# First layernorm of a spectral block: variances from the rows that the first DFT stage reads, instead of from a separate copy of x

## Chip, cores, metric

One core of one Trainium2 chip. The metric is the device time of one launch in microseconds. The kernel before takes 1050.82 us (median of 3 runs, 1050.31 to 1052.5).

## The reference

```python
def _layernorm(x, axis=-1, eps=1e-5):
    m = jnp.mean(x, axis=axis, keepdims=True)
    v = jnp.var(x, axis=axis, keepdims=True)
    return (x - m) / jnp.sqrt(v + eps)

def _A_ref(x, w_r, w_i):                 # x is (1, 2048, 1024), bf16
    X = jnp.fft.rfft2(x.astype(jnp.float32), axes=(-2, -1))
    X = X * (w_r + 1j * w_i)
    return jnp.fft.irfft2(X, s=(S, D), axes=(-2, -1)).astype(jnp.bfloat16)

x = A_x
x = x + _A_ref(_layernorm(x), A_w_r, A_w_i)
x = x + _B_ref(_layernorm(x), B_w1, B_b1, B_w2)    # two matmuls with an activation between
x = x + _A_ref(_layernorm(x), A_w_r, A_w_i)
x = x + _B_ref(_layernorm(x), B_w1, B_b1, B_w2)
```

Only the first layernorm and the first stage of the first spectral layer are changed. The transforms are matmuls with DFT matrices. The normalization by a row's standard deviation is put into the DFT matrix of the first stage: each of 128 groups of rows gets its own scaled copy of the matrix M0 (tile MN).

## The kernel before

Its prologue loads x (4 MB, tile XS, also the residual of later) and then the same rows once more in the order of the transform (tile XR, four quarters of 1 MB in pieces of 256 bytes). It takes the row statistics from XS, transposes them, scales, and runs stage one (an "eviction" copies a result of TensorE out of a pair of PSUM banks):

```python
    def first_scales(self):
        for j in range(0, 16, 4):          # row statistics, shared by VectorE and ScalarE
            n = 2 if j % 8 else 3
            for i in range(n):
                self.stats_dve(j + i)
            for i in range(n, 4):
                self.stats_act(j + i)
            self.sums_to_mv(j + n, 4 - n)
        self.root(0, 16)
        ...                                # spread, transpose on TensorE, copy back: tile RT

    def scaled(self, j):                   # 8 scaled copies of M0 for tile j, one by one
        for q in range(8):
            n = 8 * j + q
            if q % 3 == 1:
                self.op(self.act, lambda e, n=n: e.activation(self.MN.ap[:, n, :], self.M0.ap, ACT.Copy, scale=rc[:, n:n + 1]), ...)
            else:
                self.op(self.dve, lambda e, n=n: e.tensor_scalar(self.MN.ap[:, n, :], self.M0.ap, rc[:, n:n + 1], None, op0=ALU.mult), ...)

    def s1(self, li):
        for j in range(4 if not li else 0):
            self.scaled(j)
        for j in range(16):
            ps, banks, _ = self.pair()     # one of four pairs of PSUM banks
            ...                            # 8 matmuls of 128x128 per tile
            # eviction to Y: odd tiles on ScalarE, even ones on VectorE
            if not li and j + 4 < 16:
                self.scaled(j + 4)
```

Stage two begins when all 16 tiles are in Y; it runs in steps, and each of its first steps needs a block of the filter (w_r and w_i), which GpSimd loads while the steps go on.

## Time and profile before

| | before |
|---|---|
| time, median (us) | 1050.82 |
| profiled execution: time, span, granted clock | 1051.39, 1049.6, 0.966 |
| stage two starts (us from the span's start) | 46.24 |
| rest of that execution, time minus start of stage two | 1005.15 |

The page's strips of tenths (forty slices of 26 us; busy share of each engine, then the granted clock and the DMA engines) show the stretch at stake, the first two digits:

```profile
PE   0799489999999999999959967999999999999998
DVE  6898562531343100043326856426011100000111
ACT  6898263331000333300008844533300013340000
PEclk9699789999999999999989987999999999999999
```

In the first slice TensorE does nothing while VectorE and ScalarE take statistics; in the second its clock is granted at six tenths. The closer views, the chain and the durations of single instructions, are those that the prediction quotes.

### The profile page before, as it was taken

How to read it: one execution, taken by the hardware profiler on the slowest of the kernel's cores; microseconds unless marked ns; L12 is line 12 of the kernel's file. 1: busy time of each engine (PE TensorE's matmuls, PEld its weight loads, DVE VectorE, ACT ScalarE, POOL GpSimd, SP SyncE). 2: the span in 40 equal slices, each digit the busy share in tenths (PEclk: the TensorE clock that was granted, in tenths of full speed). 3: DMA queues.
4: the chain of work that ended last, by engine and by line, in shares of the span. 5: the costliest groups of instructions: out<-in, count | busy, mean ns of one | idle time of the engine just before them, and what ended most of it. 6: DMA issues, size and time to landing. Idle time of an engine off the chain costs nothing.

```text
span 1049.6 us, 14096 instructions
## 1 busy us (share of the span) xinstructions
PE 952.5 (91%) x5944; PEld 511.7 (49%) x6033; DVE 350.8 (33%) x776; ACT 336.5 (32%) x503; POOL 71.0 (7%) x114
## 2 busy tenths in 40 slices
PE   0799489999999999999959967999999999999998
PEld 0567465444444444444427746644444444444443
DVE  6898562531343100043326856426011100000111
ACT  6898263331000333300008844533300013340000
POOL 3242000000000000002421200000000000000000
PEclk9699789999999999999989987999999999999999
DMA  9779812464111221001941784145611112200000
GB/s 281 176 257 281 221 44 91 151 200 134 50 52 37 69 64 39 1 21 71 178 83 44 222 210 131 42 151 166 209 25 45 45 63 81 61 1 11 21 21 31
DMA packets 152718, 107.01 MB, mean 102 GB/s; under 512 B 74288, under 2 KB 131888, under 8 KB 152656
## 3 DMA queue, kind: packets, MB, share of 16 engines
q1 hardware_dynamic: 139936, 75.99, 25.4%
q0 software_dynamic: 9632, 28.45, 9.5%
q10 hardware_dynamic: 3088, 1.67, 0.6%
q8 instruction: 48, 0.79, 0.3%
q14 instruction: 14, 0.11, 0.0%
HBM read 80.85 MB, written 20.71 MB: 97 GB/s over the span
## 4 chain that ended last, share of the span: by engine, by line
PE 80%; DVE 9%; ACT 6%; DMA 3%; issue 1%; SPq 0%; ACTq 0%; DVEq 0%
PE PS L994 37%; PE PS L976 37%; DVE BN L459 2%; ACT ARENA L721 2%; PE PS L669 2%; DVE XS L915 1%; DVE ARENA L573 1%; DVE ARENA L790 1%; DMA u_scratch<-ARENA 1%; DMA ARENA<-u_scratch 1%; ACT ARENA L704 1%; DVE ARENA L951 1%; DVE ARENA L596 1%; PE PS L901 1%; ACT ARENA L792 1%
## 5 line engine op out<-in xcount | busy, mean ns | idle before, releaser
L976 PE MATMUL PS<-ARENA 128*128 128x512 bf16 (+1 forms) x1946 | 390.6, 360 | 10.3 <-DVE ARENA L951 7.2
L994 PE MATMUL PS<-ARENA 128*128 128x512 bf16 x1756 | 385.5, 379 | 1.9
L980 ACT ACTIVATE ARENA<-PS,B 128x512 bf16<-128x512 f32 (+1 forms) x248 | 159.8, 646 | 438.7 <-PE PS L976 438.7
L976 PEld LDWEIGHTS PS<-ARENA 128*128 128x128 bf16 x1984 | 194.2, 99 | 201.8 <-DVE ARENA L951 8.7
L994 PEld LDWEIGHTS PS<-ARENA 128*128 128x128 bf16 x1792 | 175.3, 98 | 211.5
L999 DVE TENSOR_TENSOR XS<-PS,XS 128x512 bf16<-128x512 f32 x64 | 44.3, 692 | 537.9 <-PE PS L994 537.9
L459 DVE BATCH_NORM_STATS2 BN<-XS 128x6 f32<-128x512 bf16 x104 | 67.2, 675 | 7.5 <-DMA XS<-in_A_x_dram 6.3
L915 DVE TENSOR_TENSOR XS<-PS,XS 128x512 bf16<-128x512 f32 (+1 forms) x40 | 29.1, 790 | 82.0 <-PE PS L901 82.0
L901 PE MATMUL PS<-MT,ARENA 128*128 128x32 bf16 (+1 forms) x768 | 24.5, 187 | 27.2 <-DMA ARENA<-u_scratch 23.8
L901 PEld LDWEIGHTS PS<-MT,ARENA 128*128 128x128 bf16 x768 | 23.0, 100 | 30.7 <-issue 24.7
L440 ACT ACTIVATE ARENA<-XS 128x1024 bf16<-128x1024 bf16 x24 | 25.3, 1055 | 36.4 <-DVE XS L915 31.5
L721 ACT ACTIVATE ARENA<-PS 128x1024 bf16<-128x1024 f32 x32 | 33.9, 1060 | 8.5 <-PE PS L717 8.5
L669 PE MATMUL PS<-FD,ARENA 128*128 128x256 bf16 (+1 forms) x256 | 33.6, 278 | 2.9 <-ACT ARENA L594 1.2
L750 ACT ACTIVATE ARENA<-PS 128x1024 bf16<-128x1024 f32 x32 | 33.9, 1061 | 3.7 <-PE PS L743 3.7
L249 POOL DMA_DIRECT2D xn_scratch<-ARENA x15 | 8.2, 550 | 390.7 <-DVE ARENA L498 390.7
L431 ACT ACTIVATE RS<-MV,EPS 128x1 f32<-128x1 f32 (+1 forms) x7 | 2.0, 292 | 98.5 <-DVE MV L462 96.2
L743 PE MATMUL PS<-ARENA 128*128 128x256 bf16 x256 | 33.2, 273 | 0.1
L743 PEld LDWEIGHTS PS<-ARENA 128*128 128x128 bf16 x256 | 24.5, 98 | 10.0 <-DVE ARENA L732 1.2
L725 DVE TENSOR_TENSOR ARENA<-ARENA 128x1024 bf16<-128x1024 bf16 x32 | 22.0, 687 | 21.9 <-ACT ARENA L721 21.9
L669 PEld LDWEIGHTS PS<-FD,ARENA 128*128 128x128 bf16 x256 | 24.5, 100 | 8.4 <-DVE ARENA L596 2.8
L764 PE MATMUL PS<-ARENA,BD 128*128 128x256 bf16 x192 | 25.9, 273 | 1.3 <-DVE ARENA L790 1.0
L498 DVE TENSOR_SCALAR ARENA<-XS,MV,RS 128x1024 bf16<-128x1024 bf16 x48 | 25.0, 543 | 1.0
(70 smaller groups left out, 503.8 us busy)
## 6 DMA issues: line engine op xcount, KB each, us to landing
ARENA<-in_B_w_dram SPq DMA_DIRECT2D x56, 512.0 KB, 3.9
ARENA<-in_B_w_dram SPq DMA_DIRECT2D x56, 256.0 KB, 4.2
u_scratch<-ARENA SPq DMA_DIRECT2D x14, 512.0 KB, 3.6
ARENA<-u_scratch SPq DMA_DIRECT2D x14, 512.0 KB, 5.7
XS<-in_A_x_dram SPq DMA_DIRECT2D x4, 1024.0 KB, 8.6
w_scratch<-ARENA POOLq DMA_DIRECT2D x8, 512.0 KB, 5.6
ARENA<-w_scratch POOLq DMA_DIRECT2D x8, 512.0 KB, 5.2
out_dram<-XS SPq DMA_DIRECT2D x16, 256.0 KB, 2.2
```

What stands on the lines that cost most here:

```text
L459: self.op(self.dve, lambda e: e.bn_stats(self.BN[:, j, 6 * h:6 * h + 6], self.XS[:, j, 512 * h:512 * h + 512]), reads=[self.r_xs[j]], part ...
L669: fns.append(lambda e: e.matmul(dst, at(r), FD[:, t:t + n], start=start, stop=stop))
L721: self.op(act, lambda e: e.activation(x.ap.rearrange("p a b -> p (a b)"), ps, ACT.Copy, scale=SIG), reads=banks, writes=[x.res])
L743: fns.append(lambda e, c=c, part=part: e.matmul(ps[:, c * 256:(c + 1) * 256], yk.ap[:, part, c * P:(c + 1) * P], t[:, (128, 0)[part]:(384, ...
L750: self.op(act, lambda e: e.activation(v.ap[:, :, i, :], src, ACT.Copy), reads=banks, parts=[v.res])
L764: fns.append(lambda e, dst=dst, part=part, c=c: e.matmul(dst, BD[:, c:c + P], mov(kd, part), start=(part == 0), stop=(part == 1)))
L901: fns.append(lambda e, l=l: e.matmul(ps[:, w * l:w * l + w], self.UT.ap[:, u0 + l, :], self.MT[:, 8 * lo:8 * lo + w], start=True, stop=True))
L915: self.op(self.dve, lambda e: e.tensor_tensor(xs, src, xs, ALU.add), reads=rb, parts=self.r_xs[lo:lo + nb])
L976: fns.append(lambda e, db=db, bank=bank, fl=fl: e.matmul(PS[:, bank, 0:w], wb.ap[:, db, fl * P:(fl + 1) * P], x.ap[:, db, tok], start=(db ...
L980: self.op(act, lambda e, bank=bank, ft=ft: e.activation(at.ap[:, ft, tok], PS[:, bank, 0:w], ACT.Mish, bias=self.B1[:, ft:ft + 1]), reads= ...
L994: fns.append(lambda e, i=i, ft=ft: e.matmul(PS[:, bank, :], at.ap[:, ft, t * P:(t + 1) * P], W2[ft].ap[:, h * 512:(h + 1) * 512], start=(i ...
L999: self.op(dve, lambda e: e.tensor_tensor(xs, PS[:, bank, :], xs, ALU.add), reads=[self.r_bank[bank]], writes=[self.r_xs[j]])
```

## The change

Its intent: the statistics need XS, but the rows themselves are also in XR. A block matrix of ones (BO, 8 by 8 blocks) lets TensorE add the eight pieces of each row across partitions, for the rows and for their squares. So x needn't come first, the 128 small scalings become 16 operations on VectorE, and each quarter of rows can start when it has landed. The residual x is loaded later: one megabyte behind the rows, the other three behind the first three steps of stage two (the "gate"). The core of the diff:

```diff
+                prog = (sp, self.pool, self.act)[h % 3] if q == 0 else (sp, self.pool)[h % 2]
...
+    def squares(self, q, prog):           # 4096 elements of XR squared into XQ
...
+    def sums(self, q, sq):                # 16 matmuls of 256 columns with BO, of the rows (sq=0) or their squares (1)
...
+        fns = [lambda e, i=i: e.matmul(ps, self.BO.ap, src[:, :, 8 * i:8 * i + 8], start=(i == 0), stop=(i == 15)) for i in range(16)]
...
+    def roots(self, q):                   # reduce, square, subtract on DVE; Sqrt on ACT; reciprocal on DVE
...
     def scaled(self, j):
+        self.op(self.dve, lambda e: e.tensor_tensor(self.MN.ap[:, n, :], self.M0.ap.unsqueeze(1).to_broadcast([P, 8, P]),
+                                                    self.RT.ap[:, n].unsqueeze(2).to_broadcast([P, 8, P]), ALU.mult), ...)
...
+    def s1_first(self):
...
+        self.sums(0, 0)
+        self.squares(0, dve)
+        self.sums(0, 1)
+        self.roots(0)
+        for j in range(16):
+            q = j // 4 + 1
+            if q < 4 and j % 4 == 0:
+                self.squares(q, act)
+                self.sums(q, 0)
+            self.scaled(j)
+            self.s1_mm(0, j, j % 3)
+            if q < 4 and j % 4 == 1:
+                self.sums(q, 1)
+            self.s1_evac(j, j % 3, dve if j in (13, 15) else act)
+            if q < 4 and j % 4 == 2:
+                self.roots(q)
...
+            if li == 0 and step < 3:      # in stage two
+                gate = Res("gate")
+                gate.set_w(self.pe, self.pe.count)
+                self.load_x(step + 1, [gate])
```

More of the change, by code (lines that the diff above doesn't have):

```diff
@@ L171, in make_tables @@
                 FD=np.concatenate(FD, axis=1), BD=np.concatenate(BD, axis=1), FT=by_group(FT), BT=by_group(BT),
-                ident=np.eye(P))
+                ident=np.eye(P), BO=np.kron(np.eye(16), np.ones((8, 8))))
 def to_bf16_bits(a):
@@ L307, in build @@
         self.con = {k: v.ap().bitcast(BF) for k, v in con.items()}
-        self.con["IDF"] = nc.inline_tensor(np.eye(P, dtype=np.float32), name="c_idf").ap()
         self.u_d = nc.dram_tensor("u_scratch", (8, P, 16, P), BF, kind="Internal").ap()
@@ L361, in layout @@
         K = 1024
-        self.o = dict(XR=0, Z=0, X=12 * K, T=20 * K, YK=28 * K, V=40 * K, JT=48 * K, M0=49 * K, IDF=49 * K + 256, RT=50 * K,
-                      JUNK=51 * K, WR=54 * K, YS=56 * K, UT=64 * K, MN=64 * K, Y=96 * K, XN=128 * K, U=128 * K,
+        self.o = dict(XR=0, Z=0, X=12 * K, T=20 * K, YK=28 * K, V=40 * K, JT=48 * K, M0=49 * K, BO=49 * K + 256, RT=50 * K, XQ=32 * K,
+                      ST=51 * K, WR=54 * K, YS=56 * K, UT=64 * K, MN=64 * K, Y=96 * K, XN=128 * K, U=128 * K,
                       FT=140 * K, BT=144 * K + 512, WT=self.W1_OFF)
@@ L375, in prologue, with load_small @@
         self.op(self.pool, lambda e: e.memset(self.EPS[:], 1e-5), writes=[self.r_eps, self.r_warm])
-        self.warm(ACT.Sqrt)
-        xt = self.x[0].rearrange("(t p) d -> p t d", p=P)
-        for c in range(4):
-            self.dma(sp, self.XS[:, 4 * c:4 * c + 4, :], xt[:, 4 * c:4 * c + 4, :], f"x{c}", writes=self.r_xs[4 * c:4 * c + 4])
         small = {}
-        def load_small(name, n, d):
-            b = self.alloc(name, self.o[name], [n], d)
-            self.dma(sp, b.ap, self.con[name], name.lower(), writes=[b.res])
+        def load_small(name, n, prog=sp):
+            b = self.alloc(name, self.o[name], [n])
+            self.dma(prog, b.ap, self.con[name], name.lower(), writes=[b.res])
             small[name] = b
-        load_small("M0", P, BF)
-        load_small("IDF", P, F32)
-        self.M0, self.IDF = small["M0"], small["IDF"]
         self.XR = self.alloc("XR", self.o["XR"], [P, P])
@@ L394, in prologue, with load_x @@
             for h in range(8):
-                prog = self.pool if q and h % 2 else sp
-                self.dma(prog, self.XR.ap[h:P:8, 32 * q:32 * q + 32, :], xv[h][:, 32 * q:32 * q + 32, :], f"xr{q}{prog.name}",
-                         parts=[r], reads=[self.r_xs[15]] if prog is self.pool else [])
+                prog = (sp, self.pool, self.act)[h % 3] if q == 0 else (sp, self.pool)[h % 2]
+                self.dma(prog, self.XR.ap[h:P:8, 32 * q:32 * q + 32, :], xv[h][:, 32 * q:32 * q + 32, :], f"xr{q}{prog.name}", parts=[r])
             self.r_xr.append(r)
-            if q == 2:
-                self.dma(sp, self.FD[:], self.con["FD"], "fd", writes=[self.r_fd])
-        load_small("JT", 4 * P, BF)
+            if q == 0:
+                load_small("BO", P, self.act)
+                load_small("M0", P, self.act)
+                self.warm(ACT.Sqrt)
+        self.M0, self.BO = small["M0"], small["BO"]
+        self.dma(sp, self.FD[:], self.con["FD"], "fd", writes=[self.r_fd])
+        load_small("JT", 4 * P)
         self.JT, self.r_jt = small["JT"].ap, small["JT"].res
         self.w1_next = 0
+    def load_x(self, c, after):
+        xt = self.x[0].rearrange("(t p) d -> p t d", p=P)
+        self.dma(self.sp, self.XS[:, 4 * c:4 * c + 4, :], xt[:, 4 * c:4 * c + 4, :], f"x{c}", reads=after,
+                 writes=self.r_xs[4 * c:4 * c + 4])
     def constants(self):
@@ L527, in pair, with copy @@
         return self.PS[:, 2 * i:2 * i + 2, :].rearrange("p a b -> p (a b)"), [self.r_bank[2 * i], self.r_bank[2 * i + 1]], 2 * i
-    def copy(self, prog, dst, src, reads, writes, scale=None):
+    def copy(self, prog, dst, src, reads, writes, scale=None, parts=()):
         if prog is self.act:
@@ L535, in copy @@
             fn = lambda e: e.tensor_copy(dst, src)
-        return self.op(prog, fn, reads=reads, writes=writes)
-    def first_scales(self):
-        dve, act = self.dve, self.act
-        for j in range(0, 16, 4):
-            n = 2 if j % 8 else 3
-            for i in range(n):
-                self.stats_dve(j + i)
-            for i in range(n, 4):
-                self.stats_act(j + i)
-            self.sums_to_mv(j + n, 4 - n)
-        self.root(0, 16)
-        rt = self.alloc("RT", self.o["RT"], [16, 8], F32)
-        self.op(dve, lambda e: e.tensor_copy(rt.ap, self.RS[:, 2, :].unsqueeze(2).to_broadcast([P, 16, 8])),
-                reads=self.r_rs, writes=[rt.res])
-        bank = self.r_bank[7]
-        self.group([lambda e: e.transpose(self.PS[:, 7, 0:P], rt.ap.rearrange("p a b -> p (a b)"), self.IDF.ap)],
-                   reads=[rt.res, self.IDF.res], writes=[bank])
-        self.op(dve, lambda e: e.tensor_copy(rt.ap.rearrange("p a b -> p (a b)"), self.PS[:, 7, 0:P]), reads=[bank], writes=[rt.res])
-        self.MN = self.alloc("MN", self.o["MN"], [P, P])
-        self.r_mn = [Res(f"mn{j}") for j in range(16)]
-        for r in self.r_mn:
-            r.inherit(self.MN.res)
-            r.begin()
-        self.RT = rt
@@ L564, in scaled, with open_scales @@
-    def scaled(self, j):
-        rt = self.RT
-        rc = rt.ap.rearrange("p a b -> p (a b)")
+        return self.op(prog, fn, reads=reads, writes=writes, parts=parts)
+    def open_scales(self):
+        self.XQ = [self.alloc(f"XQ{i}", self.o["XQ"] + i * 8192, [32, P]) for i in range(2)]
+        self.ST = self.alloc("ST", self.o["ST"], [4, 4, 32], F32)
+        self.RT = self.alloc("RT", self.o["RT"], [P], F32)
+        self.MN = self.alloc("MN", self.o["MN"], [P, P])
+        self.r_st, self.r_rt, self.r_mn = ([Res(f"{n}{i}") for i in range(k)] for n, k in (("st", 4), ("rt", 4), ("mn", 16)))
+        for b, rs in ((self.ST, self.r_st), (self.RT, self.r_rt), (self.MN, self.r_mn)):
+            for r in rs:
+                r.inherit(b.res)
@@ new lines, in squares @@
+    def squares(self, q, prog):
+        x, b = self.XR.ap[:, 32 * q:32 * q + 32, :], self.XQ[q % 2]
+        fn = (lambda e: e.activation(b.ap, x, ACT.Square)) if prog is self.act else (lambda e: e.tensor_tensor(b.ap, x, x, ALU.mult))
+        self.op(prog, fn, reads=[self.r_xr[q]], writes=[b.res])
+    def sums(self, q, sq):
+        bank = 6 + q % 2
+        ps = self.PS[:, bank, 256 * sq:256 * sq + 256].rearrange("p (n l) -> p n l", l=8)
+        src = self.XQ[q % 2].ap if sq else self.XR.ap[:, 32 * q:32 * q + 32, :]
+        fns = [lambda e, i=i: e.matmul(ps, self.BO.ap, src[:, :, 8 * i:8 * i + 8], start=(i == 0), stop=(i == 15)) for i in range(16)]
+        rb = self.r_bank[bank]
+        if not sq:
+            rb.begin()
+        w = list(rb.prev.items()) + self.BO.res.wait_r() + (self.XQ[q % 2].res if sq else self.r_xr[q]).wait_r()
+        t = None
+        for i, fn in enumerate(fns):
+            t = self.pe.add(fn, waits=w if i == 0 else (), inc=(i == 15))
+        self.mark(self.pe, t, reads=[self.BO.res] + ([self.XQ[q % 2].res] if sq else []), parts=[rb])
@@ new lines, in roots @@
+    def roots(self, q):
+        dve = self.dve
+        st, rst, rb = self.ST.ap[:, q], self.r_st[q], self.r_bank[6 + q % 2]
+        s1, s2, a, b = (st[:, i, :] for i in range(4))
+        rc = self.RT.ap[:, 32 * q:32 * q + 32]
+        src = self.PS[:, 6 + q % 2, :].rearrange("p (c n l) -> p c n l", c=2, l=8)
+        self.op(dve, lambda e: e.tensor_reduce(st[:, 0:2, :], src, axis=mybir.AxisListType.X, op=ALU.add), reads=[rb], writes=[rst])
+        self.op(dve, lambda e: e.tensor_tensor(a, s1, s1, ALU.mult), writes=[rst])
+        self.op(dve, lambda e: e.scalar_tensor_tensor(b, a, -1.0 / self.D, s2, ALU.mult, ALU.add), writes=[rst])
+        self.op(self.act, lambda e: e.activation(a, b, ACT.Sqrt, bias=self.EPS[:, 0:1], scale=1.0 / self.D), reads=[self.r_eps],
+                writes=[rst])
+        self.op(dve, lambda e: e.reciprocal(rc, a), reads=[rst], writes=[self.r_rt[q]])
@@ new lines, in scaled, with s1_mm @@
+    def scaled(self, j):
+        n = slice(8 * j, 8 * j + 8)
+        self.op(self.dve, lambda e: e.tensor_tensor(self.MN.ap[:, n, :], self.M0.ap.unsqueeze(1).to_broadcast([P, 8, P]),
+                                                    self.RT.ap[:, n].unsqueeze(2).to_broadcast([P, 8, P]), ALU.mult),
+                reads=[self.r_rt[j // 4], self.M0.res], writes=[self.r_mn[j]])
+    def s1_mm(self, li, j, i):
+        M, XR = self.M, self.XR
+        ps, banks = self.PS[:, 2 * i:2 * i + 2, :].rearrange("p a b -> p (a b)"), [self.r_bank[2 * i], self.r_bank[2 * i + 1]]
+        fns = []
@@ L567, in scaled @@
         for q in range(8):
             n = 8 * j + q
-            if q % 3 == 1:
-                self.op(self.act, lambda e, n=n: e.activation(self.MN.ap[:, n, :], self.M0.ap, ACT.Copy, scale=rc[:, n:n + 1]),
-                        reads=[rt.res, self.M0.res], parts=[self.r_mn[j]])
-            else:
-                self.op(self.dve, lambda e, n=n: e.tensor_scalar(self.MN.ap[:, n, :], self.M0.ap, rc[:, n:n + 1], None, op0=ALU.mult),
-                        reads=[rt.res, self.M0.res], parts=[self.r_mn[j]])
@@ L576, in s1, with s1_evac @@
-    def s1(self, li):
+            m = M[:] if li else self.MN.ap[:, n, :]
+            fns.append(lambda e, q=q, n=n, ps=ps, m=m: e.matmul(ps[:, q * P:(q + 1) * P], XR.ap[:, n, :], m, start=True, stop=True))
+        self.group(fns, reads=[self.r_xr[j // 4], self.r_m if li else self.r_mn[j]], writes=banks)
+    def s1_evac(self, j, i, prog):
+        ps, banks = self.PS[:, 2 * i:2 * i + 2, :].rearrange("p a b -> p (a b)"), [self.r_bank[2 * i], self.r_bank[2 * i + 1]]
+        self.copy(prog, self.Y.ap[:, :, 8 * j:8 * j + 8], ps.rearrange("p (q k) -> p k q", q=8), banks, [], parts=[self.Y.res])
@@ L577, in s1 @@
+    def s1_first(self):
+        self.open_scales()
         self.Y = self.alloc("Y", self.o["Y"], [P, P])
         self.Y.res.begin()
-        M, XR = self.M, self.XR
-        for j in range(4 if not li else 0):
-            self.scaled(j)
-        for j in range(16):
-            ps, banks, _ = self.pair()
-            fns = []
-            for q in range(8):
-                n = 8 * j + q
-                m = M[:] if li else self.MN.ap[:, n, :]
-                fns.append(lambda e, q=q, n=n, ps=ps, m=m: e.matmul(ps[:, q * P:(q + 1) * P], XR.ap[:, n, :], m,
-                                                                   start=True, stop=True))
-            self.group(fns, reads=[self.r_xr[j // 4], self.r_m if li else self.r_mn[j]], writes=banks)
-            src = ps.rearrange("p (q k) -> p k q", q=8)
-            dst = self.Y.ap[:, :, 8 * j:8 * j + 8]
-            if j % 2 or li and j == 8:
-                self.op(self.act, lambda e, dst=dst, src=src: e.activation(dst, src, ACT.Copy), reads=banks, parts=[self.Y.res])
-            else:
-                self.op(self.dve, lambda e, dst=dst, src=src: e.tensor_copy(dst, src), reads=banks, parts=[self.Y.res])
-            if not li and j + 4 < 16:
-                self.scaled(j + 4)
@@ L599, in s1 @@
-        for r in ([self.MN.res, self.M0.res] + self.r_xr if not li else []):
-            r.r(self.pe, self.pe.count)
-            self.XR.res.r(self.pe, self.pe.count)
+        act, dve = self.act, self.dve
+        self.sums(0, 0)
[7 more added lines that the diff above has]
+                self.sums(q, 0)
+            self.scaled(j)
+            self.s1_mm(0, j, j % 3)
[4 more added lines that the diff above has]
+                self.roots(q)
@@ new lines, in s1_first, with s1 @@
+        for r in [self.MN.res, self.M0.res, self.XR.res, self.BO.res] + self.r_xr + [b.res for b in self.XQ]:
+            r.r(self.pe, self.pe.count)
+        for r in (self.RT.res, self.ST.res, self.M0.res, self.XR.res, self.MN.res):
+            r.r(dve, dve.count)
+            r.r(act, act.count)
+    def s1(self, li):
+        if li == 0:
+            return self.s1_first()
+        self.Y = self.alloc("Y", self.o["Y"], [P, P])
+        self.Y.res.begin()
+        for j in range(16):
+            i = self.pair()[2] // 2
+            self.s1_mm(1, j, i)
+            self.s1_evac(j, i, self.act if j % 2 or j == 8 else self.dve)
@@ L640, in layer_A @@
         if li == 0:
-            self.junk = self.alloc("JUNK", self.o["JUNK"], [self.D])
-            self.first_scales()
-        if li == 0:
             self.open_tables(0)
             self.constants()
+            self.load_x(0, [])
         o, K = self.o, 1024
```

## The prediction

> **What bounds the kernel now.** The page first: TensorE is busy 91% of the span, and the two idle slices of the strip of tenths are at the start and around 540 us. The change touches only the first layernorm and the first stage of the first spectral layer, so I went from the page to the chain of waits and the timeline of the first 60 us. The chain, merged, of the kernel before:
>
> ```profile
> 0.74 5.50 DMA XS<-in_A_x_dram
> 6.27 1.30 DVE BN L459 x2
> ...
> 22.20 0.32 ACT RS L431
> ...
> 22.53 0.27 DVE RS L433
> ...
> 24.02 3.34 DVE ARENA L573 x20
> 27.36 1.13 DVE ARENA L596
> 28.49 1.62 DVE ARENA L573 x10
> ...
> 43.92 2.27 DVE ARENA L596 x2
> 46.20 0.05 issue
> 46.24 1.89 PE PS L669 x8
> ...
> 50.06 1.94 ACT ARENA L704 x2
> 52.00 0.77 ACT ARENA L885 x2
> 52.77 0.92 ACT ARENA L721
> ```
>
> Columns are start, duration, work. Until 22.8 us everything waits for row statistics (L459, bn_stats, DVE's share of them). From 24.0 to 46.2 DVE never stops: it scales the 128 copies of the DFT matrix (L573) and empties every second PSUM pair (L596). At 46.24 the second stage starts (L669), and from 50 us the chain runs through ScalarE's evictions, 0.92 us apart. So up to 46.24 the path is vector work and TensorE waits; after it each stage hangs on the one before. What the change is worth is the new start S of the second stage minus 46.24, plus any harm done later.
>
> Durations for the working come from these groups (busy us, mean ns) and from the stretches (PE, PEld, DVE, ACT, POOL busy, then granted clock, DMA share, GB/s):
>
> ```profile
> L440 ACT ACTIVATE ARENA<-XS 128x1024 bf16<-128x1024 bf16 x24 | 25.3, 1055 | 36.4 <-DVE XS L915 31.5
> L725 DVE TENSOR_TENSOR ARENA<-ARENA 128x1024 bf16<-128x1024 bf16 x32 | 22.0, 687 | 21.9 <-ACT ARENA L721 21.9
> L594 ACT ACTIVATE ARENA<-PS 128x1024 bf16<-128x1024 f32 x8 | 8.1, 1012 | 0.6 <-PE PS L588 0.6
> L596 DVE CAST ARENA<-PS 128x1024 bf16<-128x1024 f32 x8 | 9.6, 1212 | 0.0
> 20.00:25.00 5.00, 0.48 (x1) 0.18 (x1) 3.77 (x17) 2.07 (x7) 2.04 (x4) 1.00 1.18 236
> 35.00:40.00 5.00, 3.66 (x32) 3.02 (x31) 5.00 (x20) 5.00 (x15) 4.69 (x8) 0.50 1.00 134
> 50.00:55.00 5.00, 4.95 (x39) 3.64 (x38) 1.21 (x2) 4.94 (x7) 4.07 (x7) 1.00 0.65 182
> ```
>
> Two things to see. The spectral rows, read in 256-byte pieces, come in at about 240 GB/s with the DMA engines full (share 1.18). And TensorE's clock is granted at 0.50 in this phase although it is busy three quarters of the time; it comes back only after the dense start of stage two (0.68 in the microsecond from 49).
>
> **What the Trainium skill says.** "TensorE: Matmul & The Clock Gate", Part 1: the array runs at half clock until a window of some 3.4 us has been busy, and falls back after an idle one. The trace agrees and adds the threshold that matters here: 8 matmuls of 256 columns start 1.69 us apart per eight at 0.50 (0.211 each, from 46.24) and 0.87 per eight at 1.00 (0.109, from 55.98), and a window about half busy (29.2 to 32.6 us) was enough to lose the clock. "ScalarE: Activation LUTs", What ACT_TABLE_LOAD costs: 186 ns plus 0.833 ns an element; for 1024 elements 1.04, measured 1.055. "VectorE: DVE Perf Modes", The perf-mode tier table: a tensor_tensor reaches 2x in bf16 and 1x with fp32, a tensor_reduce 1x. The 0.687 us of L725 is the 2x rate; no fp32 tensor_tensor of this size is in the trace, so I take the 1x eviction's 1.21 us, next one after 1.13. "DMA: Bandwidth & Descriptors", Issuing engines are not separate DMA queues: three issuing engines save issue time only, which the full share above bears out.
>
> **The change part by part.** Removed: the 4 MB load of x ahead of the rows and all row statistics, 22 us on DVE and ScalarE, with the fp32 transpose. The 128 small scalings become 16 tensor_tensors of 1024 elements on DVE. Evictions go to ScalarE except numbers 13 and 15. Added: per quarter one squaring of 4096 elements (first on DVE, then ScalarE), 32 matmuls of 256 columns, a reduction, a root, a reciprocal. Moved: x is loaded behind the rows and in the first three steps of stage two.
>
> Costs: squaring on ScalarE 0.19 + 4096 x 0.833 ns = 3.6 us; on DVE 4 x 0.61 = 2.3 with L725's spacing. Sixteen sum matmuls 16 x 0.109 = 1.75 warm, 16 x 0.211 = 3.4 cold. Eight stage-one matmuls about 0.5 warm, 0.9 cold, plus 0.25 for the last one's tail and the semaphore. Reduction of 512 fp32 from PSUM, about 0.7 (half an eviction). The small ops up to the reciprocal 1.0 (in the kernel before 21.80 to 22.82). Scaling 1.2, next after 1.14. ScalarE eviction 0.93.
>
> *Start.* The first quarter is 1.05 MB, with two tables 1.11 MB; at 245 GB/s 4.5 us from about 2.3 us, so it is in SBUF at 7.2. Sums cold, the second sixteen half cold: 7.3 to 13.4. Reduction to 14.3, root done 15.0. First scaling 15.4. ScalarE has its first squaring (quarter 1) next in its queue: 15.0 to 18.6. Call this end X1. The other quarters land at about 11.5, 16 and 20 us and are waited for by nobody.
>
> *One quarter.* The order of instructions closes a ring. ScalarE's queue is: squaring q, three evictions, root q, one eviction, squaring q+1. From the end X of a squaring, warm: sums of squares, X+1.8; matmuls of the third group, X+2.5; its eviction, X+3.45; root (queued behind that eviction), X+3.8; reciprocal, X+4.1; the fourth scaling (queued behind the reciprocal on DVE), X+5.35; its matmuls, X+6.1; its eviction, X+7.05; squaring, X+10.6. Cold, 1.65 for sums and 0.4 to 0.5 for each matmul group more: X+13.2. ScalarE works only some 7.7 us of that; the rest is the ring. TensorE is dense for 3 us and idle for 3 us in turn, so I expect the clock to be lost and regained in each quarter: 11.6 as a mean. X2 = 30.2, X3 = 41.8.
>
> *End.* After X3: reciprocal 4.1, three scalings to 7.65, matmuls 8.4, DVE's copy 13 to 9.55, two scalings 11.9, matmuls 12.7, copy 15 to 13.9; cold 17.0. I take 14.7, so S = 56.5, which is 10.3 us later than 46.24.
>
> *Later.* The first gated megabyte of x is issued when step 0 of stage two ends, together with the filter load for step 2. Before, that load was issued at 49.57 and 50.28, landed in 3.3 to 3.7 us, at about 54.0, and its matmuls ran at 54.67: 0.6 us of slack. Sharing the DMA engines costs about 2 us there, of which ScalarE's backlog of nearly 1 us hides half: 1.0. Filter loads, tables and x in later steps fit into stretches like 58 to 61 us, where the DMA moved almost nothing. The rest of the program is shifted.
>
> Sum: 1050.8 + 10.3 + 1.0 = 1062.1.
>
> **The rivals.** *A gain.* If the quarters overlapped as intended, ScalarE's own work would be the bound: from 14.7 four roots (1.3), three squarings (10.6), 14 evictions (13.0), then DVE's last copy, S about 41.5 and 1046. For it speaks that 22 us of statistics are gone and the rows come 4 us into the program rather than last; against it the ring, which is in the order of the queues and not in the data. *All cold.* If TensorE never gets its clock, two cycles of 13.2 and the cold end give S = 18.6 + 26.4 + 17.0 = 62, and 1068; for it speaks 0.50 over 17 us before, against it the dense stretch of sums, which exceeds a window. *DMA as the bound.* If the first quarter came at 10 us because later quarters of other queues overtake it, S moves by those 3 us; the rows' total rate bounds the last quarter at 20 us, so no more. *Filter loads starved by x.* Should all three megabytes get ahead of loads for steps 2 and 3, 4 us more instead of 1.
>
> **Range and chances.** All warm and an early first quarter give S about 51.5 and 1056; a gain in the fixed hops or a squaring in another order of readiness takes off another 2 to 3. All cold with starved filter loads gives 1071. The range is 1053 to 1069. Two per cent is 21 us; a stage that lasted 46 us cannot give 21 by a reordering whose ScalarE work alone ends at 41, and a loss of 21 needs every rival of loss at once: 0.01 faster, 0.95 same, 0.04 slower.
>
> **What would show it.** In the changed profile: stage two (the matmuls on FD) starting at 54 to 59 us; squarings on ScalarE of 3.6 us spaced by 10.5 to 13; ScalarE waiting for TensorE before the third and fourth eviction of each quarter, about 3 us or more a quarter; DVE waiting for the root before its reciprocal; a scaling of 1.2 us (0.7 would mean the 2x rate); clock 0.5 and 1.0 in turn; the matmuls of the filter for step 2 a microsecond or so late. The prediction is wrong if squarings come every 8 us, or if the first sums start much before 7 us, or if a sum matmul, whose moving operand is read in 16-byte runs, takes another time than 0.109 and 0.211.

## The result, and the profile after

The changed kernel took 1064.51 us (median of 4 runs, 1061.64 to 1067.35) beside 1050.99 for the kernel before; the ratio is 1.0127, 95% interval 1.0097 to 1.0156. (Ratios and intervals are from the runs of the same rounds, so not quite the ratio of the quoted medians. For two kernels below they also differ from the ratio of the plain means of all listed executions, which is then given.) In the profiled execution (1064.61 us) stage two started at 57.34, 11.1 us later than before, and the rest took 1007.27, 2.1 us longer.

The chain of the changed kernel, merged: start, duration, work.

```profile
5.34 12.28 DMA ARENA<-in_A_x_dram
17.62 0.02 issue
17.64 3.62 ACT ARENA L554
...
21.32 1.92 PE PS L562 x16
23.24 0.46 PE PS L599 x8
...
23.72 1.02 ACT ARENA L533
24.74 0.22 ACT ARENA L582
...
24.98 0.35 DVE ARENA L584
25.34 1.09 DVE ARENA L588
...
26.47 1.05 PE PS L599 x8
27.52 0.02 issue
27.54 0.02 ACT ARENA L533
...
28.46 3.62 ACT ARENA L554
...
39.28 3.62 ACT ARENA L554
...
57.34 1.89 PE PS L707 x8
...
61.37 7.51 DMA ARENA<-in_A_w_i_dram
```

L554 is the squaring, L562 the sums, L599 stage one's matmuls, L533 the eviction, L582 the root, L584 the reciprocal, L588 the scaling. The reader sees the ring that the prediction wrote down, hop for hop: squaring, sums of squares, third group's matmuls, its eviction, root, reciprocal, fourth scaling, its matmuls, its eviction, squaring. It closes after 10.82 us, twice (17.64, 28.46, 39.28). The chain begins, however, not with a root but with a load: SyncE's seventh piece of rows, the last of its half of quarter 1, issued at 5.34, took 12.28 us. And behind stage two's start the chain runs through another load, of the filter.

The waits say the same, by who waits and for what (total us, times, longest):

```profile
ACT ARENA L554 <- DMA ARENA<-in_A_x_dram: 1.8, 1, 1.8
PE PS L912 <- DMA ARENA<-in_A_w_i_dram: 3.1, 1, 3.1
```

The second is TensorE's wait for the filter block of step 2. These are the landing times of that filter tensor's loads from 40 to 75 us, first of the kernel before, then of the changed kernel:

```profile
DMA to landing us min/median/max: 3.5/3.9/6.3
```

```profile
DMA to landing us min/median/max: 6.0/7.5/8.2
```

The changed kernel was run once more later, unedited, for the scatter of its profile:

> The changed kernel once more, unedited, beside the others of this call: 1064 to 1065, as in its first runs; it shows how far profile and time of one and the same kernel differ between runs (landing of the first rows and of quarter 1, wait for the filter).

It took 1063.86 us (1063.46 to 1066.29; ratio 1.0134, interval 1.0121 to 1.0147). In its profile the squarings came 10.82 and 10.40 apart, stage two started at 58.42 and the wait for the filter was 1.74 us. So the start of stage two scatters by a microsecond and that wait by more than one, between executions of one kernel.

### The profile page after: what moved, and what is told of

The parts are those of the page before. It is cut to its first block, busy times and chain, and to the rows that moved or that the text cites. A ratio compares the mean times of both kernels' runs of the same rounds, so it can differ in the third digit from the quotient of the medians.

```text
span 1062.5 us, 14272 instructions
## 1 busy us (share of the span) xinstructions
PE 966.3 (91%) x6071; PEld 522.9 (49%) x6160; DVE 341.3 (32%) x678; ACT 326.0 (31%) x443; POOL 72.8 (7%) x117
## 4 chain that ended last, share of the span: by engine, by line
PE 76%; DVE 7%; DMA 6%; ACT 5%; issue 3%; POOL 2%; SPq 0%; ACTq 0%; DVEq 0%; POOLq 0%
PE PS L1018 36%; PE PS L1036 32%; POOL ARENA L249 2%; PE PS L707 2%; DMA xn_scratch<-ARENA 1%; DVE XS L957 1%; DMA ARENA<-in_A_x_dram 1%; ACT ARENA L554 1%; DMA u_scratch<-ARENA 1%; ACT ARENA L533 1%; DVE ARENA L828 1%; ACT ARENA L759 1%; PE PS L781 1%; DMA ARENA<-u_scratch 1%; DVE ARENA L993 1%
## 5 line engine op out<-in xcount | busy, mean ns | idle before, releaser
L461 DVE BATCH_NORM_STATS2 BN<-XS 128x6 f32<-128x512 bf16 x84 | 54.7, 677 | 1.2
L759 ACT ACTIVATE ARENA<-PS 128x1024 bf16<-128x1024 f32 x32 | 33.3, 1042 | 8.6 <-PE PS L755 8.6
L788 ACT ACTIVATE ARENA<-PS 128x1024 bf16<-128x1024 f32 x32 | 33.3, 1041 | 4.1 <-PE PS L781 4.1
L781 PE MATMUL PS<-ARENA 128*128 128x256 bf16 x256 | 33.2, 273 | 0.5 <-DMA ARENA<-c_bt 0.4
L562 PE MATMUL PS<-ARENA 128*128 128x256 bf16 x128 | 19.4, 319 | 14.7 <-DMA ARENA<-in_A_x_dram 12.0
L533 ACT ACTIVATE ARENA<-PS 128x1024 bf16<-128x1024 f32 x23 | 22.4, 1027 | 25.4 <-PE PS L599 25.3
```

Source lines behind the costliest of these rows:

```text
L461: self.op(self.dve, lambda e: e.bn_stats(self.BN[:, j, 6 * h:6 * h + 6], self.XS[:, j, 512 * h:512 * h + 512]), reads=[self.r_xs[j]], part ...
L533: fn = (lambda e: e.activation(dst, src, ACT.Copy)) if scale is None else \
L759: self.op(act, lambda e: e.activation(x.ap.rearrange("p a b -> p (a b)"), ps, ACT.Copy, scale=SIG), reads=banks, writes=[x.res])
L781: fns.append(lambda e, c=c, part=part: e.matmul(ps[:, c * 256:(c + 1) * 256], yk.ap[:, part, c * P:(c + 1) * P], t[:, (128, 0)[part]:(384, ...
L788: self.op(act, lambda e: e.activation(v.ap[:, :, i, :], src, ACT.Copy), reads=banks, parts=[v.res])
```

## The experiments

Each run was timed in five rounds against the kernel before on the same chip. My theory after the first result had four parts: the order of the instructions around the ring (main part), the half clock of TensorE, the starved filter load, the late quarter 1. Each rival says that its part is hidden behind the others.

**One part at a time: order.** The root goes behind the fourth eviction instead of ahead of it, so that neither has to wait for the other's chain:

```diff
-            if q < 4 and j % 4 == 2:
+            if q < 4 and j % 4 == 3:
                 self.roots(q)
```

> One line: the root of the next quarter (reduction, root, reciprocal) is issued after the fourth eviction of a quarter, not after the third. No work is added or taken away. Ring theory (squaring, three evictions, root, reciprocal, fourth scaling, its matmuls, its eviction, next squaring): the fourth scaling no longer hangs behind the reciprocal, so the spacing of ScalarE's squarings falls from 10.8 us to about 8, stage two starts at about 50.5 instead of 57.3, and the time falls by about 7 us to 1057 to 1058. Rival (the work itself of ScalarE and DVE sets the quarter): spacing and time unchanged, 1064. Rival (TensorE's half clock sets the quarter): spacing falls by less than 1 us.

1060.71 us (1055.61 to 1061.36), ratio 1.0088 (1.0071 to 1.0105): a gain of 3.8, half of what I had expected; stage two started at 55.39, not 50.5. The squarings came 8.11 us apart once (17.82 to 25.93), which confirms the ring, and then 9.77. ScalarE's timeline and TensorE's (start, duration, then the idle time before and what ended it) show why:

```profile
25.93 3.62 ACT L554 ACTIVATE ARENA<-ARENA 128x4096 bf16<-128x4096 bf16 x1
29.44 1.94 ACT L533 ACTIVATE ARENA<-PS 128x1024 bf16<-128x1024 f32 x2
33.66 1.94 ACT L533 ACTIVATE ARENA<-PS 128x1024 bf16<-128x1024 f32 x2 [2.28 <-PE PS L599]
```

```profile
29.61 3.57 PE L562 MATMUL PS<-ARENA 128*128 128x256 bf16 x16
```

The sums of squares took 3.57 us where the changed kernel's took 1.92, because they now fall into a stretch at half clock, and ScalarE waited 2.28 us for the tile behind them instead of 0.63. The tail grew too: the matmuls of the last tiles came in two groups of 16 that took 2.17 us each. Two cycles of 8.11 would have saved 5.4 us; the second cycle and the tail (16.1 us from the end of the last squaring to stage two, where the changed kernel needed 14.4) took 3.3 of that back, by this reading through the clock; the runs that hold the clock test it below. (In the profiled executions only 2.0 us of the gain lie in the start of stage two. The wait for the filter was 1.7 us instead of 3.1, which is within its scatter.)

**x not gated.** All four loads of x are issued behind the constants; the gate is gone.

```diff
-            self.load_x(0, [])
+            for c in range(4):
+                self.load_x(c, [])
...
-            if li == 0 and step < 3:
-                gate = Res("gate")
-                gate.set_w(self.pe, self.pe.count)
-                self.load_x(step + 1, [gate])
```

> All four megabytes of x are issued right behind the small tables at about 24 us, with no wait for stage two; the DMA engines stand idle from 37 to 57 us in the changed kernel. Theory (the gated loads of x starve the filter load of step 2, TensorE waits 3.1 us there): stage two still starts at about 57, the wait for the filter goes from 3.1 us to below 0.5, the time falls by 2 to 3 us to about 1062. Rival (the loads are late whatever x does, or ScalarE's backlog hides the wait): within 0.5 us of 1064.5.

1061.95 us (1061.08 to 1062.57), ratio 1.0108 (1.0095 to 1.0121), as expected. Stage two started at 57.21, as in the changed kernel, and TensorE no longer waited for the filter. The landing times of the filter's loads from 40 to 75 us in this kernel:

```profile
DMA to landing us min/median/max: 3.8/4.5/5.0
```

So it was the gated x that starved them.

**Rows dealt by quarter.** Of quarter 1, seven of eight pieces go to GpSimd's queue, of quarter 2 five, and SyncE gets five of quarter 3:

```diff
-  ... if q == 0 else (sp, self.pool)[h % 2]
+  ... if q == 0 else (sp, self.pool)[h > 0 if q == 1 else h % 3 > 0 if q == 2 else h > 4]
```

> The same 32 row loads, with more of quarters 1 and 2 issued from GpSimd (7 of 8, 5 of 8) and more of quarter 3 from SP. Theory (SP's queue gets only half of the service that GpSimd's gets, so its four loads of quarter 1 land at 17.6 us, and ScalarE's first squaring waits 1.8 us for them): quarter 1 lands at about 13, the first squaring starts at 15.9 right behind the root, all later stages are 1.8 us earlier, time about 1062.7. Rival (the rows arrive at one total rate, and quarter 1 is late because quarter 0 was): first squaring still at about 17.6, no change.

1063.5 us (1062.38 to 1064.67), ratio 1.0123 (1.011 to 1.0137): no gain clear of the noise. ScalarE's timeline:

```profile
16.68 0.32 ACT L582 ACTIVATE ARENA<-ARENA,EPS 128x32 f32<-128x32 f32 x1 [11.62 <-DVE ARENA L581]
16.91 3.60 ACT L554 ACTIVATE ARENA<-ARENA 128x4096 bf16<-128x4096 bf16 x1
...
24.63 1.02 ACT L533 ACTIVATE ARENA<-PS 128x1024 bf16<-128x1024 f32 x1 [2.30 <-PE PS L599]
```

The wait for rows is gone: the squaring stands right behind the root. But the first rows landed at 9.74 instead of 8.67 in this execution, and the first cycle took 12.23 us, with a wait of 2.30 for TensorE where it had been 0.63: the sums of squares of that quarter took 3.35 us. In this execution, then, the wait that was removed came back as half clock; one execution does not show that it has to. Nor need the landing at 9.74 be the edit's doing: it was between 8.67 and 9.82 in the six profiles that deal the rows as the changed kernel does.

**All three together.**

> The three edits together. If the three losses lie one after the other on the path they add: 7 + 2.5 + 1.8 = 11.3 us, so about 1053, stage two from about 48.7. If one hides another, less: above 1055.

1057.89 us (1056.41 to 1058.74), ratio 1.0068 (1.0054 to 1.0081). From the changed kernel's 1064.51 the single gains are 3.8, 2.6 and 1.0 (the last within the noise), together 7.4; measured 6.6. The parts as measured nearly add up; what failed was the 11.3 that I had expected of them. 7 us of the loss remained. Stage two started at 54.09; the squarings were 9.75 and 8.11 apart. In the cycle of 9.75 the sums of squares took 3.25 us, in that of 8.11 they took 1.92.

**Holding the clock.** To test the clock by itself, matmuls of 512 columns whose result is overwritten are put where TensorE idles, into the PSUM bank that the next real matmuls start afresh:

```diff
+    def busy(self, i, n):
+        ps = self.PS[:, 2 * i, :]
+        w = self.r_xr[0].wait_r() + self.r_bank[2 * i].wait_w()
+        for k in range(n):
+            self.pe.add(lambda e: e.matmul(ps, self.XR.ap[:, 0, :], self.XR.ap[:, 0:4, :], start=True, stop=True), ...)
...
             self.scaled(j)
+            self.busy(j % 3, {3: 10, 7: 10, 11: 10, 14: 9}.get(j, 0))
             self.s1_mm(0, j, j % 3)
...                                        # and busy(1, 5) ahead of stage two
```

> The changed kernel as it is, with idle-time matmuls of 512 columns whose result is thrown away: ten ahead of the first-stage matmuls of tiles 3, 7 and 11, nine ahead of tile 14, five ahead of stage two. Theory (TensorE's half clock lengthens what lies on the path: sums of squares, the last tiles' matmuls, the first matmuls of stage two): the sums of squares of quarters 2 and 3 take under 2.2 us where the changed kernel took over 3, spacing of the squarings 10.4, stage two starts about 1.5 to 2 us earlier and runs its first microseconds at full clock: about 1062.0, 2.5 less than the changed kernel. Rival (the clock of these few matmuls is hidden, or the added matmuls stand in the way of the real ones): no gain or a loss, 1064 to 1067.

1064.16 us (1063.68 to 1065.39), ratio 1.0128 (1.0115 to 1.0141): no gain, the rival's number. But the profile doesn't show the rival's mechanism. The granted clock was 1.00 from 24 us on to the filter's wait; the second cycle fell to 10.40; the first 24 matmuls on FD (stage two's table) and the filter matmuls among them were through at about 60.5 us, where the changed kernel needed until about 62.4. Then TensorE waited:

```profile
67.21 1.03 PE L922 MATMUL PS<-ARENA 128*128 128x256 bf16 x4 [2.61 <-DMA ARENA<-in_A_w_i_dram]
```

and the next matmuls on FD stood at 70.89, against 71.13 in the changed kernel. My reading was that the filter's landing took the gain. The trace says it more exactly: the filter had landed 1.7 us earlier too (TensorE went on at 67.21, not 68.93), but after the wait the clock was 0.50 from 67 to 70 us, where the changed kernel had kept 1.00 behind a longer wait, so that the stretch up to the next matmuls on FD took 3.68 us instead of 2.20. So in this execution the wait took the gain by way of the clock. (Stage two itself started only 0.3 us earlier, at 57.05, not the 1.5 to 2 that I had expected: the first rows landed at 9.82 in this execution, and the first cycle took 11.05.) Whether the gain appears when the wait is gone can be tested: the same matmuls in the kernel without the gate.

> The kernel of w1 (the changed kernel with idle-time matmuls) with x not gated, as in e2. Theory (w1 did run stage one's end and stage two's first matmuls at full clock and won 2 us there, but TensorE then waited for the third filter block, which came when the DMA queues let it, so the time did not move): without that wait the 2 us stay, about 1060 where e2 alone had 1061.95, and TensorE shows no wait for the filter. Rival (full clock in these stretches is worth nothing, whatever the filter does): as e2, 1061.5 to 1062.5.

1059.01 us (1057.56 to 1063.59), ratio 1.0079 (1.0066 to 1.0092); the plain means of all six executions, the slow one included, give 1.0088. So the four kernels form a square, in ratios to the kernel before:

| | gated x | x not gated |
|---|---|---|
| no added matmuls | 1.0127 and 1.0134 | 1.0108 |
| added matmuls | 1.0128 | 1.0079 |

Added matmuls are worth nothing with the gate and 2.9 thousandths (3.0 us) without it (2.0 by the plain means); taking the gate away is worth about 2 thousandths alone and 5 (4) with them. That the added matmuls gain without the gate is clear of the noise by the intervals, and denies the rival of this run. That they gain more there than with the gate, so that the two causes hide each other, is likely and not shown: each ratio is uncertain by 1.3 thousandths, hence the difference of the two gains (1.4 to 3.0) by about 2.6. (The profile of this kernel fell on its slowest execution, 1063.59 us, in which the clock was lost all the same, 0.51 from 33 to 36 us; TensorE had no wait for the filter in it. So the square rests on the times.) I had expected 1060.

The same on top of all three parts, with other counts (six ahead of tiles 4 and 8, fourteen ahead of 12, nine ahead of 14, five ahead of stage two):

> The kernel of e4 (root behind the fourth eviction, rows dealt by quarter, x not gated) with idle-time matmuls: six ahead of tiles 4 and 8, fourteen ahead of tile 12, nine ahead of tile 14, five ahead of stage two. Theory (half clock is what e4 still loses): squarings 8.1 us apart in every cycle instead of 9.75 and 8.11, the third quarter's sums of squares under 2.2 us instead of 3.37, stage two starts at 50 to 51 instead of 54.1, and the time is about 1053, with 1052 if the first matmuls of stage two gain too. Rival (the clock is not on the path): 1057 to 1059 as e4.

1055.11 us (1053.52 to 1056.46), ratio 1.004 (1.0028 to 1.0051). Stage two started at 50.78, as expected, 3.3 earlier than without; the time fell by 2.8, to 2 us above what I had expected. The first cycle was still 9.56 us, since the clock in it was 0.70 (18 to 21 us): no added matmuls stand ahead of that quarter's sums. The second was 8.11.

**Taking the ring apart.** In the changed kernel one squaring has to wait for four evictions. Here each is issued right behind the root before it, evictions follow in threes, and all evictions are ScalarE's; rows by quarter and no gate. The order (S scale, M matmuls, E evict; Q square; T sums, .0 of rows and .1 of squares; R root):

```text
T0.0 V0 T0.1 R0 Q1 T1.0 S0 M0 S1 M1 S2 M2 T1.1 E0 E1 E2 S3 M3 R1 Q2 T2.0 S4 M4 S5 M5 T2.1
E3 E4 E5 S6 M6 S7 M7 R2 Q3 T3.0 S8 M8 T3.1 E6 E7 E8 S9 M9 S10 M10 S11 M11 R3 E9 E10 E11
S12 M12 E12 S13 M13 E13 S14 M14 E14 S15 M15 E15
```

> Rows dealt by quarter and x not gated as in e4, and the ring taken apart: each ScalarE squaring is issued right behind the root before it, ahead of that quarter's evictions, the evictions follow in threes while VectorE scales and TensorE sums, and all evictions are ScalarE's. Theory (the order of instructions around the ring, squaring to sums to root to scaling to eviction to squaring, is the cost, and ScalarE's own work of 16 evictions at 1.2, 3 squarings at 3.6 and 3 roots is the next bound: about 32 us from the first root at 16.7): stage two starts at 49 to 51 with some waits, the time is 1051 to 1054. Rival (the sums at half clock keep the cycle at about 9.8 whatever the order): stage two at 54 to 56, 1057 to 1060.

1050.22 us (1045.56 to 1051.65), ratio 0.9985 (0.9969 to 1.0001; 0.9989 by the plain means): level with the kernel before, better than expected. Stage two started at 47.03, and 7.02 us was the spacing of the second and third squaring. Only the first cycle, at half clock (0.50 from 21 to 24 us), took 9.62. The rival, that the clock keeps the cycle near 9.8 whatever the order, fell for the kernel as a whole; in the one cycle that did run at half clock it was about right.

With twenty matmuls on a constant tile before the first rows land, and some between quarters, around the last tiles and ahead of stage two:

> The kernel of b1 with idle-time matmuls: twenty on a constant tile before the first rows land, and some to hold the clock between the quarters, around the last tiles and ahead of stage two. Theory (order and clock together are all of what the change loses): ScalarE is without gaps from the first root on, stage two starts at 46.5 to 49 (46.2 in the kernel before), the time is 1047 to 1051: level with the kernel before or a little under it. Rival (the clock is not held by such matmuls, or they collide with the real ones): as b1 or above it.

1048.14 us (1046.34 to 1051.04), ratio 0.9977 (0.9964 to 0.9989). Stage two started at 43.59. The first sums ran warm, so the first root stood at 13.99 us. Beside the run with all three parts and added matmuls, this also tests the order with the clock held in both: 1.004 against 0.9977, 6.6 us, of which the first root (15.68 there) accounts for 1.7 and the first cycle, cold in part there, for 1.4. What the order is worth is therefore not the clock in disguise.

A refinement of it: the second quarter's sums of squares go ahead of tile 2's matmuls (T1.1 before S2 M2), the last eviction to VectorE.

> The kernel of b2 with two moves: the second quarter's sums of squares ahead of tile 2's matmuls instead of behind them (they waited 0.85 us for a tile that VectorE had not scaled), and the last tile's eviction on VectorE. Theory: the wait of 1.2 us ahead of the second root falls to about 0.7, the last eviction ends 0.4 us earlier, stage two starts at about 42.7 instead of 43.6: about 1047.3, 0.9 under b2. Rival (the loads of the next rows then bind): as b2, 1048.

1046.37 us (1045.42 to 1048.98), ratio 0.9968 (0.9956 to 0.998), so it beats both kernels: the one before by a third of a per cent, the changed one (1063.86 in the same rounds) by 1.6 per cent. Stage two started at 43.21, less than half of the expected gain there; against the run before it the ratio is 0.9 thousandths lower, and the intervals overlap. A line of ScalarE's timeline of it, then a cycle of its chain:

```profile
28.53 0.32 ACT L582 ACTIVATE ARENA<-ARENA,EPS 128x32 f32<-128x32 f32 x1 [0.45 <-DVE ARENA L581]
```

```profile
21.83 3.51 ACT ARENA L554
...
25.39 1.94 PE PS L562 x16
...
27.35 0.70 DVE ARENA L579
...
28.53 0.02 ACT ARENA L582
...
28.75 3.61 ACT ARENA L554
```

In a cycle of 7.02 us ScalarE idles 0.45, so its own work is close to the bound. But it is not yet the bound: what closes the cycle is a shorter ring, squaring, sums of squares, reduction (L579), root, next squaring, without the evictions and the scaling. The first kernel in the new order has the same ring and the same 7.02.

**The control.** The added matmuls could help the kernel before as well. It got four ahead of each tile from the fifth on, and five ahead of stage two (the same helper, in its s1).

> The kernel before, with four idle-time matmuls ahead of each first-stage tile from the fifth on and five ahead of stage two. Its stage one runs at half clock from 32.6 to the start of stage two. Theory (what b2 has over the kernel before is partly the clock, which the kernel before can have too): full clock through stage one, the last two tiles' matmuls 0.8 us shorter, the first 24 matmuls and the filter of stage two about 1.7 us shorter: about 1048.5, level with b2. Rival (VectorE and ScalarE bind stage one, and stage two's start gives nothing, or the added matmuls delay real ones): 1050 to 1052.

1050.18 us (1048.86 to 1052.45) beside 1050.05, ratio 1.0001 (0.9989 to 1.0014): the rival's number. In the profile the granted clock reads 1.00 throughout (not so the pace: the first 32 matmuls took 3.49 us from 25.20, 0.87 for eight, where later ones took 0.45; the column does not show this cold start) and stage two started at 46.34, as before; its first 24 matmuls on FD ended 1.5 us sooner. That execution took 1048.9, but three of six took over 1050.7, so no gain is shown, and where the 1.5 us went in the slower ones is open. It does show that the margin of the last two kernels over the one before is not the added matmuls alone.

All profiled executions in one table; "rest" is the execution's time minus the start of stage two. The profiled execution is not always a typical one: it was the slowest of its kernel for "rows by quarter" and "not gated, matmuls added", the fastest for "all three, matmuls added" and "new order, matmuls added".

| kernel | median us | ratio | stage two starts | rest |
|---|---|---|---|---|
| before | 1050.82 | 1 | 46.24 | 1005.2 |
| before, matmuls added | 1050.18 | 1.0001 | 46.34 | 1002.6 |
| after, two profiles | 1064.51, 1063.86 | 1.0127, 1.0134 | 57.34, 58.42 | 1007.3, 1005.7 |
| root behind fourth eviction | 1060.71 | 1.0088 | 55.39 | 1005.0 |
| x not gated | 1061.95 | 1.0108 | 57.21 | 1004.4 |
| rows by quarter | 1063.5 | 1.0123 | 58.01 | 1006.7 |
| all three | 1057.89 | 1.0068 | 54.09 | 1004.0 |
| after, matmuls added | 1064.16 | 1.0128 | 57.05 | 1006.6 |
| not gated, matmuls added | 1059.01 | 1.0079 | 58.49 | 1005.1 |
| all three, matmuls added | 1055.11 | 1.004 | 50.78 | 1002.7 |
| new order | 1050.22 | 0.9985 | 47.03 | 1004.2 |
| new order, matmuls added | 1048.14 | 0.9977 | 43.59 | 1002.8 |
| the same, refined | 1046.37 | 0.9968 | 43.21 | 1003.2 |

The start of stage two explains most of it: it spans 15 us over these kernels, the rest under 5.

## Why the prediction was right, by its steps

- **The frame.** That only the start of stage two and harm behind it count was right, and the sum too: 1062.1 predicted, 1064.51 and 1063.86 measured. The start was predicted at 56.5 and came at 57.34.
- **The ring.** "The order of instructions closes a ring" was right, in every hop, and it is shown: another order took the squarings from 10.82 to 7.02 us apart and the loss to nothing (with the gate off and the rows dealt anew, which by themselves were worth about 3.6 us). Its size was between warm and cold as I had written: 10.82, against 10.6 warm and a mean of 11.6 taken. Too pessimistic by 0.8 a cycle, 1.6 in all. The clock did come and go in each quarter, but the sums at half clock were those of the rows, hidden behind the squaring, and cost nothing; on the ring only the fourth tile's matmuls were cold, 0.4 us. The run with added matmuls confirms that size, and so does the second profile of the changed kernel: where these matmuls were warm, the cycle was 10.40. The costs came as estimated: squaring 3.62, reduction 0.69, scaling 1.14, sixteen sums 1.75 from start to start (17.67 to 19.42), 0.109 each, so the 16-byte runs that the prediction feared did no harm.
- **The start.** Rows in SBUF at 7.2 was 1.5 too early (8.67; the sum written there, 4.5 from 2.3, even gives 6.8). "The other quarters land at about 11.5, 16 and 20 us and are waited for by nobody" was the step that failed: quarter 1 was complete at 17.62, and ScalarE waited 1.8 us. I had taken one rate for all queues; from 9.5 to 15.5 us GpSimd's queue moved 1.09 MB and SyncE's 0.34. The rival "DMA as the bound" had this mechanism, other queues' later quarters overtaking, but saw it for the first quarter only. Together the end of the first squaring was 21.26, not 18.6: 2.7 late, which the ring's 1.6 and an end of 14.4 (14.7 predicted) made up for all but 0.8. The total owes some of its closeness to errors of opposite sign.
- **The end.** 14.7, chosen between 13.9 warm and 17.0 cold, was right here, 14.4; in the second profile it was 16.1.
- **Later.** The mechanism was right, x ahead of the filter's step 2, and its size was not: 1.0 predicted, 2.1 by the table's rest (0.6 in the second profile), with a wait of 3.1 and 1.7. The load took 7.5 us instead of 3.7, so sharing cost 3.8 us and not 2.
- **The rivals.** "A gain", with stage two at 41.5 and 1046, was computed from ScalarE's own work and rejected because of the ring. With the ring shortened, and with matmuls added, the numbers came near it: 43.21 and 1046.37. "All cold" did not happen. "Filter loads starved" happened in part.
- **The clock's threshold, and slips.** That a window about half busy loses the clock is what the kernel before shows (1.71 us of work in the 3.4 from 29.2), but it is no rule: in the new order without added matmuls 1.17 us of work in the 3.4 from 40.17 kept it at 1.00. Three slips changed nothing: 4 x 0.61 is 2.44 (that squaring took 2.29), the mean of 10.6 and 13.2 is 11.9, and the strip has a third thin slice of TensorE, its fifth digit.

## What to carry to other kernels

When work is cut into pieces that are to overlap, write down for one piece which instruction of each queue stands ahead of which, and follow the loop: if it closes through all engines, its length is a sum and not a maximum, and no engine will look busy. Removing one wait tells little while another stands behind it: here full clock was worth nothing measurable while a starved load was in the way, and 2 to 3 us without it, though that contrast is not clear of the noise. Loads that are put off "until later" meet other loads there; look at what they will share the DMA engines with.

## What the Trainium skill lacked or had wrong

- "DMA: Bandwidth & Descriptors", Queues, rings and completion order: it says that each engine goes round the queues a packet at a time, and drains a whole packet before it switches. From 9.5 to 15.5 us, with rows in 256-byte pieces on both queues, GpSimd's moved 1.09 MB in 393 packets (2.8 KB each) and SyncE's 0.34 MB in 1364 (250 bytes each). Equal turns for two queues that always have work would give equal numbers of packets, so the trace does not show the rule as it stands. What the page lacks is the consequence for pieces that small: by bytes the share was 3.2 to 1, and SyncE's seventh load of 128 KB took 12.28 us, while all that GpSimd's fifteen moved was through by 16.5. That the packets are the cause was not tested by itself.
- The same page gives no figure for what a bulk load does to a smaller one issued with it: the filter's loads (w_i, 256 KB each) took 7.5 us (median) beside gated x (1 MB each), 4.5 without and 3.9 in the kernel before.
- "TensorE: Matmul & The Clock Gate", Part 1: half clock and its return agree (sixteen matmuls of 256 columns 1.92 us warm, up to 3.58 cold). It names short idles between groups of matmuls as a way to lose the clock, but has no busy share for it, and these traces give none either: in the kernel before TensorE was busy 2.1 of each 3 us from 35 to 44 us and the clock stayed at 0.50, in the new order 1.17 of 3.4 us kept it at 1.00.
- No page tells of throwaway matmuls in the gaps of a kernel. They held the clock at 1.00 in the kernel before and in the last order, but not in every execution (0.51 from 33 to 36 us in the one of the ungated kernel).
